# Linear attention and a gated MLP in one hand-ordered kernel: the third pair's alpha is loaded fifth of nine, and every engine's order is new

## The chip, the cores and the metric

The kernel runs on one core of a Trainium2 chip. The metric is the device time of one execution in microseconds (us); lower is better. TensorE (PE) multiplies matrices into PSUM, VectorE (DVE) and ScalarE (ACT) read PSUM, GpSimd (POOL) works on SBUF alone here, SyncE (SP) issues DMAs. Each engine takes its instructions in the program's order and waits on semaphores.

## The reference, cut to what matters

Eight heads of width 48, four batches of 768 tokens. A state of 48 x 48 per head is decayed by alpha on its rows and gets an outer product added, token by token; then all heads of a token form a row of 384 for an MLP whose gate is h cos(h).

```python
for t in range(S):
    state = alpha[:, :, t, :, None] * state + np.einsum('bhd,bhe->bhde', k[:, :, t], v[:, :, t])
    y[:, :, t] = np.einsum('bhd,bhde->bhe', q[:, :, t], state)
...
h = x @ w_in
g = h * np.cos(h)
return (g @ w_out).astype(np.float32)
```
x has 3072 rows of 384, d_ff is 2048.

## The kernel before, in words

**Tiles.** 256 tokens form a pair of chunks of 128; there are 12 pairs, J0 to J11, three to a batch. All matmuls take bf16. Two tokens stand on each partition (e is the token's parity), 64 partitions are one chunk (c).

**Steps of a pair.** `load` (L102) brings a (alpha), k, q, v from HBM on SP's queue, 384 KB each. For J0 to J2, `ln` (L140) takes the logarithm of alpha on ACT; `cums0` (L175) and `cums` (L159) sum logarithms up to each token with triangular matrices on TensorE, into two banks of PSUM; `icp` (L190) and `exps` (L195) take the exponentials of minus and plus these sums. From J3 on, `mula` (L148) first multiplies the two tokens' alphas on POOL, so only `cums` is needed (into a bank with the tag x), `sub` (L181) on DVE makes the other sum, and one step `eb`, the session (L203), does all four exponentials and the logarithm of the next pair. `sk` (L211) and `sq` (L215) multiply k and q by the exponentials, on POOL, or on DVE where the plan has :D. `trans` (L252) transposes the products on TensorE, `evT` (L262) copies them to SBUF (DVE, or ACT with :A), `scores` (L267) multiplies them, `mask` (L275) on DVE applies the causal mask. `outer` (L282), `add` (L299) and `state` (L309) carry the state on; `decay` (L241) makes the chunk's decay on POOL. `castv` (L219) makes v bf16 on POOL; `vpe` and `vev` (L231, L238), or `vst` with four DMAs (L222), put it into the order that `yT` needs. `yT` (L316) adds state and scores to y, transposed, and `evy` (L343) evicts it as the MLP's input.

**The MLP.** `m1` (L354) makes a quarter u of h on TensorE: 12 matmuls into two banks. `sin` (L363) takes the cosine on ACT, `gate` (L371) multiplies on DVE, `m2` (L376) multiplies by w_out in four parts for each half c of the pair, `evo` (L394) evicts, `store` (L404) writes 192 KB out.

**Resources that tie steps together.** PSUM has three slots of two banks (tag h: sums of J0 to J2, transposes, scores, outer products, y, quarters of h, in the order of their steps), one bank x (sums from J3 on, vpe), one bank o (m2's result and the filler). A step waits until the reader of the slot's last content is done. ACT has one set of functions for logarithm and exponential and another for the cosine; a change costs an ACT_TABLE_LOAD (L137, L366). The weights come on POOL's DMA queue, which casts them: w1 in two halves (L122: quarters 0 and 1, 2 and 3), w2 in four quarters (L127), one for each part of m2. `idle` (L411) is filler: matmuls of zeros into bank o.

**The order.** `PLAN` (L432) holds for each step and pair a due time in ns; the steps are issued in the order of these times (L502 to L515), which fixes each engine's order and each queue's. Nothing waits for the times themselves; a planner wrote them. `IDLE` (L500) places filler. `GATES` (L99) names a load that must wait for a step: alpha of J2 waits for the last matmul of yT J1, and all loads behind it on SP wait with it.

Of the kernel before, what the change touches and what calls it, by code (L numbers as in the profile page):

```python
# [16 lines left out]
def kernel(  # L17
# [11 lines left out]
    B, H, S, D = q.shape  # L29
# [64 lines left out]
    w1 = [consts.tile([C, KT, DF // 2], BF, tag=f"w1{r}", name="w1") for r in range(2)]  # L94
    w2 = consts.tile([C, NF, DM], BF, tag="w2", name="w2")

    a_sb, kqv, cp_sb, icp_sb, qkT_sb, A_sb, c2_sb = {}, {}, {}, {}, {}, {}, {}
    xT, gsb = {}, {}
    GATES, AFTER = {("a", 2): ("yT", 1)}, {}  # L99
    src = {"a": alpha, "k": k, "q": q, "v": v}  # L100

    def load(nm, J):  # L102
# [308 lines left out]
    def idle(n):  # L411
# [18 lines left out]


    PLAN = {  # L432
# [66 lines left out]
    }  # L499
    IDLE = [(1201, 9), (6413, 9), (9413, 4), (10803, 4), (11874, 5), (13469, 5), (15483, 4), (16533, 2), (17668, 1), (23484, 1)]  # L500

    order = []  # L502
    for key, line in PLAN.items():
        kind, *rest = key.split()
        for J, word in enumerate(line.split()):
            if word != "-":
                t, _, eng = word.partition(":")
                args = [J] + [int(x) if x.isdigit() else x for x in rest] + [{"A": "ACT", "D": "DVE", "P": "POOL"}[x] for x in eng]
                order.append((int(t), len(order), kind, args))
    for t, n in IDLE:  # L510
        order.append((t, len(order), "idle", [n]))
# [34 lines left out]
```

## Time and profile before

| | us |
|---|---|
| median of 3 runs | 186.08 (185.83 to 186.11) |
| the profiled execution | 185.2 |
| its span (first to last instruction) | 183.4 |
| first MLP matmul (m1 J0, quarter 1) | 20.62 |
| last matmul's group starts | 179.47 |
| TensorE busy in the span | 177.0 (96%) |
| filler on TensorE, 44 matmuls | 12.9 |
| ACT busy, table loads among it | 129.4, 18 of 1.28 each |

The page of the profile counts an engine as busy while an instruction of its own runs; matmuls overlap, and their ends are modelled, so starts are compared below. In a line of the time line stand the start, the time until the group's end, engine, source line, operation, what it writes and reads, the count, and in brackets the engine's idle time before it and what ended it. A line of waits has the total, the count and the longest. In a row of the table of stretches, the figures before (x...) are the busy us of PE, its weight loads, DVE, ACT and POOL; then the granted clock, the DMA engines' share and GB/s.

### The profile page before, as it was taken

The numbers are of one execution on the slowest core, as the hardware profiler recorded it, in microseconds if no ns is written. First come the engines' busy times: TensorE is split into PE (matmuls) and PEld (weight loads), VectorE is DVE, ScalarE is ACT, GpSimd is POOL, SyncE is SP. The second block draws the span as 40 slices with busy tenths as digits, with TensorE's granted clock in tenths as the row PEclk, the third lists the DMA queues.
The fourth block names the chain that finished last, engine by engine and source line by source line (L and its number), as shares of the span: only waits on it lengthen the run. The fifth ranks groups of instructions, "written<-read, shape, count | busy, mean of one in ns | idle before, by whom it ended". The sixth has DMA issues, their size and how long they took to land.

```text
span 183.4 us, 5752 instructions
## 1 busy us (share of the span) xinstructions
PE 177.0 (96%) x2473; PEld 132.8 (72%) x2473; DVE 128.4 (70%) x174; ACT 129.4 (71%) x168; POOL 80.3 (44%) x114
## 2 busy tenths in 40 slices
PE   7999999989999999989999999999999999999993
PEld 2444889664797876966789769776786796788772
DVE  7268879179889696689539985988569759074650
ACT  3665769698599989869798999659947173551531
POOL 5357500568687756562991099345075111000000
DMA  6999999999988999989228970571652300020122
GB/s 151 261 261 198 215 211 249 246 267 287 247 197 201 262 242 230 256 189 285 59 46 211 282 212 4 138 176 32 168 162 65 98 5 0 5 86 4 43 86 86
DMA packets 57801, 29.47 MB, mean 161 GB/s; under 512 B 50992, under 2 KB 56496, under 8 KB 57776
## 3 DMA queue, kind: packets, MB, share of 16 engines
q1 hardware_dynamic: 56256, 25.86, 57.7%
q0 software_dynamic: 1376, 3.15, 9.1%
q8 instruction: 19, 0.31, 0.7%
q10 hardware_dynamic: 144, 0.10, 0.2%
q14 instruction: 6, 0.05, 0.1%
HBM read 25.17 MB, written 4.72 MB: 163 GB/s over the span
## 4 chain that ended last, share of the span: by engine, by line
PE 87%; ACT 8%; DMA 2%; DVE 1%; issue 1%
PE h_ps L360 34%; PE o_ps L389 31%; PE y_ps L339 5%; PE A_ps L273 4%; PE idle_ps L415 3%; PE T_ps L259 3%; PE U_ps L290 2%; DMA a<-in_alpha_dram 2%; ACT c_sb L366 2%; ACT lna L142 2%; PE o_last L383 1%; ACT cp L201 1%; PE cums_h L156 1%; PE cums L156 1%; ACT icp L193 1%; ACT L137 1%
## 5 line engine op out<-in xcount | busy, mean ns | idle before, releaser
L371 DVE TENSOR_TENSOR gsb<-h_ps,c_sb 128x1024 bf16<-128x1024 f32 x48 | 58.1, 1222 | 24.1 <-ACT c_sb L366 22.8
L366 ACT ACTIVATE c_sb<-h_ps,halfpi 128x1024 bf16<-128x1024 f32 x48 | 52.8, 1113 | 24.1 <-PE h_ps L360 21.7
L389 PE MATMUL o_ps<-w,gsb 128*128 128x384 bf16 x368 | 67.4, 327 | 1.1 <-DVE gsb L371 0.8
L360 PE MATMUL h_ps<-xT,w 128*128 128x256 bf16 x576 | 67.1, 273 | 0.1
L360 PEld LDWEIGHTS <-w 128*128 128x128 bf16 x576 | 62.4, 114 | 2.7 <-issue 0.4
L389 PEld LDWEIGHTS <-gsb 128*128 128x128 bf16 x368 | 33.8, 98 | 22.1 <-DVE gsb L371 1.4
L312 POOL TENSOR_TENSOR un<-us,c 128x384 bf16<-128x384 f32 x20 | 16.7, 835 | 42.5 <-DVE us L304 27.6
L278 DVE TENSOR_TENSOR A_sb<-A_ps,msk 128x1024 bf16<-128x1024 f32 x24 | 28.8, 1216 | 2.7 <-PE A_ps L273 2.7
L217 POOL TENSOR_TENSOR qh<-q,cp 128x384 bf16<-128x384 f32 x21 | 20.9, 1004 | 12.3 <-PE A_ps L273 8.1
L213 POOL TENSOR_TENSOR kh<-k,icp 128x384 bf16<-128x384 f32 x17 | 17.0, 1006 | 0.7 <-ACT icp L193 0.7
L150 POOL TENSOR_TENSOR a<-a 128x384 f32<-128x384 f32 x9 | 9.0, 1000 | 15.0 <-DMA a<-in_alpha_dram 14.8
L415 PE MATMUL idle_ps<-zeros 128*128 128x512 bf16 x44 | 12.9, 428 | 1.2 <-DVE zeros L52 1.2
L265 DVE COPY qkT<-T_ps 128x1024 bf16<-128x1024 bf16 x14 | 9.3, 682 | 5.0 <-PE T_ps L259 5.0
L137 ACT ACT_TABLE_LOAD x9 | 11.5, 1283 | 0.9 <-PEq L530 0.7
L142 ACT ACTIVATE lna<-a 128x768 bf16<-128x768 f32 x12 | 10.1, 845 | 2.8 <-DMA a<-in_alpha_dram 2.8
L265 ACT COPY qkT<-T_ps 128x1024 bf16<-128x1024 bf16 x10 | 9.8, 1017 | 2.9 <-PE T_ps L259 1.6
L220 POOL CAST vp<-v 128x768 bf16<-128x768 f32 x12 | 9.9, 825 | 4.1 <-DMA v<-in_v_dram 4.1
L366 ACT ACT_TABLE_LOAD x9 | 11.5, 1283 | 0.2
L401 ACT COPY o_sb<-o_ps 128x384 f32<-128x384 f32 x12 | 5.8, 482 | 8.2 <-PE o_ps L389 8.2
L304 DVE TENSOR_TENSOR us<-U_ps,un 128x384 f32<-128x384 f32 x16 | 8.8, 551 | 2.5 <-PE U_ps L290 1.4
L350 ACT CAST xT<-y_ps 128x384 bf16<-128x384 f32 x14 | 7.6, 597 | 4.0 <-PE y_ps L339 3.4
L401 DVE COPY o_sb<-o_ps 128x384 f32<-128x384 f32 x11 | 6.1, 552 | 6.2 <-PE o_ps L389 6.2
(70 smaller groups left out, 153.1 us busy)
## 6 DMA issues: line engine op xcount, KB each, us to landing
a<-in_alpha_dram SPq DMA_DIRECT2D x12, 384.0 KB, 5.9
q<-in_q_dram SPq DMA_DIRECT2D x12, 384.0 KB, 5.4
k<-in_k_dram SPq DMA_DIRECT2D x12, 384.0 KB, 5.9
v<-in_v_dram SPq DMA_DIRECT2D x12, 384.0 KB, 5.9
out_dram<-o_sb SPq DMA_DIRECT2D x23, 192.0 KB, 2.1
vs<-vp SPq DMA_DIRECT2D x36, 64.0 KB, 2.5
w<-in_moe_w_in_dram POOLq DMA_DIRECT2D x2, 768.0 KB, 9.8
w<-in_moe_w_out_dram POOLq DMA_DIRECT2D x4, 384.0 KB, 9.1
```

What stands on the lines that cost most here:

```text
L137: nc.scalar.preload_act_table_set("natural_log_exp_and_others")
L142: nc.scalar.activation(out=lna_t[J % NL][:, :, :, 0:D].rearrange("p e h d -> p h e d"), in_=a_sb.pop(J), func=AF.Ln)
L213: eng.tensor_tensor(out=kh_t[J % NQ][:, e, :, 0:D], in0=kqv["k", J][:, :, e], in1=icp_, op=ALU.mult)
L217: eng.tensor_tensor(out=qh_t[J % NQ][:, e, :, 0:D], in0=kqv["q", J][:, :, e], in1=cp, op=ALU.mult)
L265: copy(out=qkT_sb[J][:, c], in_=T_ps[J][:, c].rearrange("r n e s -> r n (e s)"))
L278: nc.vector.tensor_tensor(out=A_sb[J][:, c].rearrange("s a p t -> s (a p) t"), in0=A_ps.pop((J, c)).rearrange("s a p t -> s (a p) t"), in1 ...
L312: nc.gpsimd.tensor_tensor(out=u, in0=U_sum.pop(n), in1=c2_sb[J][:, :, c].unsqueeze(3).to_broadcast([C, NP, 2, D]), op=ALU.mult)
L360: nc.tensor.matmul(h_ps[J, u][:, f, :], cols, xT[J][:, kk, :], start=(kk == 0), stop=(kk == KT - 1))
L366: nc.scalar.activation(out=c_sb[J, u], in_=h_ps[J, u], func=AF.Sin, bias=halfpi, scale=1.0)
L371: nc.vector.tensor_tensor(out=gsb[J][:, u * FW : (u + 1) * FW], in0=h_ps.pop((J, u)), in1=c_sb.pop((J, u)), op=ALU.mult)
L389: nc.tensor.matmul(o_ps[J, c][:, 0:DM], gsb[J][:, ft, c * C : (c + 1) * C], w2[:, ft], start=(ft == 0), stop=(ft == NF - 1))
L415: nc.tensor.matmul(idle_ps[0], zeros[:, 0:C], zeros, start=True, stop=True)
```

## The change

Only the order table changes: `PLAN`, `IDLE` and `GATES`. No function and no shape changes.

- Alpha of J2 is loaded fifth of nine loads at the start (a0, a1, q0, k0, a2, v0, k1, q1, v1); before, eight loads came first, and a2 with the later ones. Its logarithm, sums and exponentials stand among those of J0 and J1.
- The gate on yT J1 moves to alpha of J3.
- `ln` J3 now stands on ACT between two cosines of pair J1; before, it stood in the session of J2.
- TensorE has 41 matmuls of filler in place of 44; the one behind the first m1 is gone.
- Both halves of y of J0 and J1, and of some later pairs, are evicted next to each other on one engine.
- All later steps get new due times; some products and copies change engine (`sq` on DVE 11 times in place of 3, `sk` 9 in place of 7, `evo` 11 in place of 12).

The lines that the prediction speaks of, cut:

```diff
-    GATES, AFTER = {("a", 2): ("yT", 1)}, {}
+    GATES, AFTER = {("a", 3): ("yT", 1)}, {}
...
-        "load a": "750 1890 23566 24136 33206 39906 42906 54176 55781 57281 67081 74982",
+        "load a": "750 2205 4425 24496 25066 37693 43693 45193 55293 56793 62293 70470",
...
-        "w1": "11430 12280 45741 34391",
-        "w2": "19412 18392 21867 16762",
+        "w1": "12930 13780 14800 45594",
+        "w2": "18398 20198 24245 21048",
...
-        "ln": "4660 7660 31941 34779 - - - - - - - -",
-        "cums0": "5565 8565 33114 - - - - - - - - -",
+        "ln": "4660 6160 12304 35108 - - - - - - - -",
+        "cums0": "5565 7065 13604 - - - - - - - - -",
...
-        "icp 0": "6470 10760 33634 - - - - - - - - -",
-        "icp 1": "8400 10000 35519 - - - - - - - - -",
-        "exps 0": "6085 10375 34009 - - - - - - - - -",
-        "exps 1": "6845 9615 34394 - - - - - - - - -",
-        "eb": "- - - 40521 47404 57439 67428 82609 86208 101733 107581 125601",
+        "icp 0": "7285 8430 15799 - - - - - - - - -",
+        "icp 1": "8805 11929 15424 - - - - - - - - -",
+        "exps 0": "6900 7660 15039 - - - - - - - - -",
+        "exps 1": "8045 13044 14654 - - - - - - - - -",
+        "eb": "- - - 39444 47093 58049 68038 83323 88148 102153 108001 126061",
...
-        "m1 3": "23912 36576 53619 60672 74283 97913 108778 110096 134625 143522 159692 171168",
-        "sin 3": "25430 38196 55137 62190 75801 99431 111127 112135 136143 145040 161210 172686",
+        "m1 3": "24842 34044 54229 61582 76211 98333 109238 111209 134990 143887 160057 171533",
+        "sin 3": "26360 37142 55747 63100 77729 99851 111547 112727 136508 145405 161575 173051",
...
-    IDLE = [(1201, 9), (6413, 9), (9413, 4), (10803, 4), (11874, 5), (13469, 5), (15483, 4), (16533, 2), (17668, 1), (23484, 1)]
+    IDLE = [(1201, 9), (6413, 2), (7383, 14), (11727, 1), (12377, 4), (15372, 5), (16939, 5), (20459, 1)]
```

108 rows, old and new, of the table PLAN are left out of this document.

## The prediction, made before the changed kernel had run

> **What bounds the kernel now.** I read the page's busy times first, then the table of stretches, then TensorE's waits and time line, and then the landings of the DMAs that TensorE's first work needs.
>
> ```profile
> PE 177.0 (96%) x2473; PEld 132.8 (72%) x2473; DVE 128.4 (70%) x174; ACT 129.4 (71%) x168; POOL 80.3 (44%) x114
> ```
> ```profile
> 5.30:20.60 15.30, 15.09 (x238) 7.86 (x238) 9.66 (x14) 9.26 (x18) 8.27 (x12) 1.00 1.20 235
> ...
> 24.50:38.40 13.90, 13.90 (x117) 11.52 (x116) 8.24 (x10) 10.77 (x14) 4.13 (x5) 1.00 1.06 242
> 38.40:50.70 12.30, 11.16 (x225) 7.11 (x223) 10.87 (x15) 9.44 (x17) 8.46 (x11) 1.00 1.13 268
> 50.70:80.50 29.80, 29.79 (x417) 24.35 (x414) 24.09 (x29) 27.06 (x32) 21.20 (x26) 1.00 0.96 231
> ```
> TensorE (first busy figure) is full from 5.3 us on, but until 20.6 us much of it is filler (idle, L415). From the first MLP matmul at 20.62 us it only stops in the stretch 38.4 to 50.7. The DMA engines (share above 1.0 in the first 50 us) are just as full there. So the end is set by three things: when the first MLP matmul starts, how much work stands behind it, and the waits behind it. The granted clock is 1.00 in each row.
>
> ```profile
> 20.62 2.78 PE L360 MATMUL h_ps<-xT,w 128*128 128x256 bf16 x24
> ...
> 24.23 0.39 PE L415 MATMUL idle_ps<-zeros 128*128 128x512 bf16 x1
> 24.55 0.71 PE L360 MATMUL h_ps<-xT,w 128*128 128x256 bf16 x5
> ```
> ```profile
> PE o_ps L389 <- DVE gsb L371: 0.8, 1, 0.8
> PE T_ps L259 <- DVE gsb L371: 0.5, 1, 0.5
> PE o_ps L389 <- ACT o_sb L401: 0.3, 1, 0.3
> ```
> These three waits fall at 40.84, 80.95 and 44.69 us. The first and third come from pair 2's own session of logarithm and exponentials on ACT, which waits for alpha:
> ```profile
> 31.12 1.28 ACT L137 ACT_TABLE_LOAD   x1
> 32.79 0.84 ACT L142 ACTIVATE lna<-a 128x768 bf16<-128x768 f32 x1 [0.39 <-DMA a<-in_alpha_dram]
> 34.73 0.49 ACT L193 ACTIVATE icp<-cums_h 128x384 f32<-128x384 f32 x1 [1.09 <-PE cums_h L168]
> ...
> 37.12 1.28 ACT L366 ACT_TABLE_LOAD   x1
> 38.41 1.11 ACT L366 ACTIVATE c_sb<-h_ps,halfpi 128x1024 bf16<-128x1024 f32 x1
> ```
> The cosine of pair 1 at 38.41 waits behind that session, its gate on DVE behind it, and m2 at 40.84 behind the gate.
>
> **The change, step by step.** Pairs are J0 to J11; m1(J,u) and m2 are the MLP's matmuls.
>
> *1. The first m1: later by 0.6.* The eight input loads of before land at 4.39, 5.88, 7.39, 8.89, 10.40, 11.91, 13.43 and 14.98: one each 1.51 us. In the new order (a0 a1 q0 k0 a2 v0 k1 q1 v1) k1, q1 and v1 land one place later, v1 at 16.49. POOL casts v0 before it issues w1; v0 comes at 11.91 instead of 10.40, so w1 is issued 1.51 later too, and the weights queue behind inputs that end 1.51 later. In before the first half of w1 took 8.4 us from its issue at 11.22:
> ```profile
> w<-in_moe_w_in_dram POOLq DMA_DIRECT2D x1, 768.0 KB, 8.4
> ```
> so it landed at 19.64, and now at 21.15. TensorE's own chain is ready before that: fillers cost 0.213 us each plus 0.1 per group (9 of them: 6.16 to 8.26), which puts trans J0 at 10.2, cums J1 at 10.8, ln J2 at 11.9 to 12.6, its sums at 13.15 (when the exponential of J1 frees their bank), trans J1 at 16.2 (q1 lands at 14.98, then two DVE products of 0.55), yT J0 at 17.95 (18.66 in before), its evictions until 19.85, outer J1 at 19.9 (bank of y), vpe and a filler until 20.9. So m1(0,1) starts at 21.2 instead of 20.62: **+0.58**, the margin of the other chain being 0.3. m1(0,3) follows m1(0,1) by 3.93 in before (matmul, cosine, gate, then the bank is free); the filler at 24.23 stands inside that wait, so taking it out is worth 0.
>
> *2. Pair 2's sums before the first m1.* cums0 and cums of J2 occupy TensorE from 33.70 to 34.55. They now stand where filler stood: **-0.85**. The load that J2's alpha waited for (the gate on yT J1) now holds J3's alpha; the same number of loads stands ahead of J3's k, q and v, so these land where they did (41.3, 42.8, 45.3). J2's q, k, v land 1.5 later (37.1, 38.5, 39.9); trans J2 needs them at 40.9, so nothing waits. All loads behind on SP keep their distance.
>
> *3. The waits from 24.5 to 52 us.* Before, measured by starts against neighbours: 0.79, 0.29 and 0.31 (at 40.84, 42.44 and 44.69), 1.39 in sum. After:
> - m2(0,0) part 2 needs the last quarter of w2. It landed at 31.68, now 33.2, and TensorE asks for it at 33.0: 0.2 to 0.4, I take 0.3 (bounds 0 and 1).
> - m1(1,3) moves ahead of J0's last m2, so nothing covers that eviction: 36.50 (m2) to 37.91 (copy ended) in before, 1.45 from start to a free bank, less the 0.65 of the m2 itself: 0.8. In before m1(1,3) hid it.
> - J3's alpha lands at 34.4, POOL's product ends at 35.5, ln at 36.3, cosine (1,3) at 37.6, session J3 at 39.95 to 42.3. vpe J2 needs the bank that these exponentials read until 41.65, and comes at 41.85: 0 as long as the two waits above stand; 0.4 if they go, so they trade places.
> - From there ACT is the tight engine: two evictions of J2, two of T, session J4 at 47.2 to 49.5, two of y until 50.55; m1(2,1) at 50.6, where TensorE would be at 50.4: 0.2.
>
> Sum 1.3 against 1.39: **-0.09**. At J2's second m1 that gives 51.9 instead of 52.29.
>
> On one term a rule speaks against the change. A table load takes 1.28 us, and each order has 18. The Trainium skill, ScalarE: Activation LUTs, "Table sets: the hidden batching unit", says to do all functions of one set before switching. J3's logarithm now stands alone between two cosines and needs two loads for 0.85 us of work. By the rule, ACT would be 2.6 us earlier with it elsewhere and the 0.2 above would be 0; by the row the sum stands.
>
> The weights meet the loads of J3, J4 and q2, issued at 24.8 as before, while 1.5 us more of the weights is left. In before, from 24 to 30 us the input queue moved 512 packets and 0.20 MB beside 1.10 MB of weights. The Trainium skill, DMA: Bandwidth & Descriptors, "Queues, rings and completion order", has each engine go round its queues packet by packet; those counts agree. By it the last weights lose 0.65 us more of sharing, some 0.1 us, and the sum is -0.56 instead of -0.66.
>
> *4. The rest, 52 us to the end.* Same instructions in another order; table loads 9 and 9 in both. Behind J2's second m1 the old order changes 44 times between the MLP's matmuls or sums and attention's, the new one 42 times; a change costs 0.09 in the trace (m2 to m2 0.65, m2 to scores 0.74), so -0.2. The wait at 80.95 came from POOL's product for J6 ending at 80.90, behind a cast that waited for v6 until 76.40:
> ```profile
> 76.40 0.82 POOL L220 CAST vp<-v 128x768 bf16<-128x768 f32 x1 [2.09 <-DMA v<-in_v_dram]
> ...
> 79.89 1.00 POOL L213 TENSOR_TENSOR kh<-k,icp 128x384 bf16<-128x384 f32 x1
> ```
> ```profile
> 80.95 0.41 PE L259 MATMUL T_ps<-ident_bf,kh 64*128 64x64 bf16 x16 [0.46 <-DVE gsb L371]
> ```
> (The wait is put down to the gate that ended at 80.94 as well; by the order of the slots, trans took the one that the gate before it had freed at 79.63.) Now DVE makes that product, so 0.46 goes. But with the order new everywhere, waits of this size appear at places that I can't see: from none to two of them, 0 to 1.0 us. So this stretch is worth -0.66 to +0.34; I take 0.36 of new waits, a little less than the one that goes: **-0.3**.
>
> Sum: +0.58 - 0.85 - 0.09 - 0.3 = -0.66. The profiled execution took 185.2 (span 183.4 and 1.8 around it): 184.5. The median of 186.08 lies 0.9 above that execution, so **185.4**; own range 185.0 to 185.7.
>
> **Rivals.**
> - *Nothing gained: new waits take it back.* vpe's wait of 0.4 for the bank of J3's session stands beside the others instead of in their place, and the stretch behind 52 us is near its upper end: -0.36 + 0.4 + 0.3, 186.4. For it: ACT is at 27.1 of 29.8 from 50.7 us on, with little room. Against: in before trans J6 is the only step behind 52 us with a wait in the profile.
> - *Slower: the weights come later than the shift of 1.51.* The place is the one line of DMA: nine loads, w1, w2, alpha of J3. 0.2 MB of w1 got through beside the last inputs in before; without that, at 0.2 MB per us, w1 lands 1.0 later, and the first m1, m2's last quarter, and the chain from J3's alpha through ln and the session move with it. It decides from 1.0 us on: 0.66 is eaten up, and over 0.2% slower follows. At 2 us: 187.4; at 1.1: 186.5. For it: the weights already end late (31.68). Against: issue and inputs move by the same 1.51.
> - *More gained: no new waits behind 52 us, and none of 0.2 at m1(2,1):* -0.36 - 0.2 - 0.66, 184.9.
> - *It doesn't do what it says:* ln J2 late, sums after the first m1. Its alpha lands at 10.4, ACT is free at 11.9; I give it nothing.
>
> **How the numbers follow.** Forecast 0.45, more gained 0.12, nothing gained 0.23, slower 0.20. 0.2% is 0.37 us, about what a measurement of this kernel can tell from no change. Forecast and more gained lie below 185.7: faster 0.57. Of nothing gained and the edge of slower, 0.22 is within; 0.21 slower. The range takes in both sides: 184.6 to 187.0.
>
> **What would show it.** The first h_ps at 21.2, released by w's DMA; no sums of J2 after it; the cosine (1,3) alone between two table loads at 36 to 39; a wait of 0.8 for the copy of o near 39; J2's first m1 near 50.6; trans J6 without wait. Wrong would be: a first h_ps later than 22, m2 waiting for w2 by over 1 us, or over 1 us of new waits behind 52 us.

## The result: 0.8% faster, twice what was forecast

| | median us (range, runs) | ratio to before on the same chip, 95% interval |
|---|---|---|
| before, beside the first run of after | 185.78 (184.87 to 186.11, 6) | |
| after | 184.04 (183.84 to 184.52, 6) | 0.992 [0.9891, 0.9948] |
| after, second time | 183.85 (183.32 to 185.51, 9) | 0.9916 [0.9889, 0.9943] |
| after, third time | 183.86 (183.48 to 184.06, 6) | 0.9932 [0.9918, 0.9946] |

The forecast was 185.4 with a range from 184.6 to 187.0; the time came out below the range. The profiled execution of after took 184.12 (span 182.3). The lines that answer to those of before, first the page's busy times:

```profile
PE 175.4 (96%) x2467; PEld 132.6 (73%) x2470; DVE 134.8 (74%) x183; ACT 129.9 (71%) x169; POOL 71.4 (39%) x104
```
and the table of stretches of after:

```profile
5.30:20.60 15.30, 14.36 (x239) 8.20 (x242) 10.07 (x15) 9.83 (x21) 7.39 (x11) 1.00 1.22 238
...
24.50:38.40 13.90, 13.74 (x152) 11.53 (x141) 9.53 (x10) 11.74 (x12) 3.93 (x6) 1.00 1.12 240
38.40:50.70 12.30, 11.64 (x230) 7.46 (x228) 10.67 (x14) 11.66 (x21) 9.02 (x11) 1.00 1.18 261
50.70:80.50 29.80, 29.80 (x414) 24.43 (x413) 24.58 (x30) 27.69 (x34) 13.99 (x18) 1.00 1.00 240
```
TensorE is busy 1.6 us less in all, 0.73 of it between 5.3 and 20.6 us, where it has less filler and stops more. Between 38.4 and 50.7 us it now stops for 0.66 instead of 1.14. Where the MLP begins, its time line of after says:

```profile
20.35 0.52 PE L290 MATMUL U_ps<-vp,kh 64*128 64x96 bf16 x16 [0.32 <-ACT xT L350]
20.80 0.35 PE L235 MATMUL vs_ps<-vp,ident_bf 64*64 64x384 bf16 x2
21.30 2.88 PE L360 MATMUL h_ps<-xT,w 128*128 128x256 bf16 x24 [0.16 <-issue]
...
25.24 2.03 PE L360 MATMUL h_ps<-xT,w 128*128 128x256 bf16 x17 [0.16 <-DVE gsb L371]
```
The first m1 stands at 21.30. TensorE's waits of after that answer to those shown, and the largest new one behind the start:

```profile
PE o_ps L389 <- DVE o_sb L401: 0.6, 1, 0.6
PE A_ps L273 <- DVE gsb L371: 0.5, 1, 0.5
```
The wait of 0.8 for a gate at 40.84, that of 0.3 for a copy on ACT and that of trans J6 are gone. The first line is the copy of o that nothing covers (m2 at 39.38), the second the scores of J5 at 83.09. ACT's time line of after, where pair 2's session had been:

```profile
33.78 1.28 ACT L137 ACT_TABLE_LOAD   x1
35.27 0.84 ACT L142 ACTIVATE lna<-a 128x768 bf16<-128x768 f32 x1 [0.20 <-POOL a L150]
36.13 1.28 ACT L366 ACT_TABLE_LOAD   x1
37.42 1.11 ACT L366 ACTIVATE c_sb<-h_ps,halfpi 128x1024 bf16<-128x1024 f32 x1
38.56 1.28 ACT L137 ACT_TABLE_LOAD   x1
39.85 0.52 ACT L193 ACTIVATE icp<-cp 128x384 f32<-128x384 f32 x1
```
J3's logarithm stands alone between two loads, the cosine (1,3) behind it, and the session of J3 starts at 39.85 (39.95 was forecast).

**A common zero.** Executions differ in when the first transfer lands: the first alpha at 4.37 to 4.67 us, and with it all that follows. Counted from that landing, the profiled executions read:

| | first alpha lands | first m1 | J2's second m1 | trans J6 | last m2 group |
|---|---|---|---|---|---|
| before | 4.39 | 16.23 | 47.90 | 76.56 | 175.08 |
| before, second time | 4.60 | 16.22 | 47.89 | 76.86 | 175.44 |
| after | 4.67 | 16.63 | 46.90 | 77.29 | 173.74 |
| after, second time | 4.63 | 16.67 | 46.92 | 77.31 | 173.73 |
| after, third time | 4.54 | 16.63 | 46.96 | 77.36 | 173.79 |

(trans J6 has another place in the new order.) After is the same three times within 0.07; the gain is 1.34 against the first execution of before and 1.70 against the second. The medians give 1.3 to 1.6 (0.0068 to 0.0084 of about 185.5). The spans on the pages (183.4 and 182.3) show only 1.1, because the profiled before had its first alpha 0.28 earlier than the profiled after.

### The profile page after: what moved, and what is told of

Read it like the earlier page. It is cut to its first block, busy times and chain, and to the rows that moved or that the text cites. A ratio compares the mean times of both kernels' runs of the same rounds, so it can differ in the third digit from the quotient of the medians.

```text
span 182.3 us, 5756 instructions
## 1 busy us (share of the span) xinstructions
PE 175.4 (96%) x2467; PEld 132.6 (73%) x2470; DVE 134.8 (74%) x183; ACT 129.9 (71%) x169; POOL 71.4 (39%) x104
## 4 chain that ended last, share of the span: by engine, by line
PE 77%; ACT 11%; DVE 6%; DMA 2%; issue 2%; ACTq 0%
PE h_ps L360 29%; PE o_ps L389 28%; PE y_ps L339 5%; DVE gsb L371 5%; PE idle_ps L415 4%; ACT c_sb L366 3%; PE A_ps L273 3%; PE T_ps L259 3%; DMA a<-in_alpha_dram 2%; PE U_ps L290 2%; ACT L366 2%; PE o_last L383 1%; ACT L137 1%; ACT lna L142 1%; PE cums_h L156 1%
## 5 line engine op out<-in xcount | busy, mean ns | idle before, releaser
L312 POOL TENSOR_TENSOR un<-us,c 128x384 bf16<-128x384 f32 x20 | 16.8, 838 | 46.2 <-DVE us L304 36.9
L217 POOL TENSOR_TENSOR qh<-q,cp 128x384 bf16<-128x384 f32 x13 | 13.8, 1063 | 13.3 <-ACT cp L201 12.2
L213 POOL TENSOR_TENSOR kh<-k,icp 128x384 bf16<-128x384 f32 x15 | 14.9, 1007 | 2.4 <-ACT icp L193 1.0
L415 PE MATMUL idle_ps<-zeros 128*128 128x512 bf16 x38 | 11.1, 439 | 1.4 <-DVE halfpi L77 1.2
L217 DVE TENSOR_TENSOR qh<-q,cp 128x384 bf16<-128x384 f32 x11 | 6.8, 629 | 5.4 <-DMA q<-in_q_dram 5.3
L273 PE MATMUL A_ps<-qkT 48*128 48x128 bf16 x192 | 9.0, 217 | 0.7 <-DVE gsb L371 0.5
```

The costliest lines, as they stand in the source:

```text
L213: eng.tensor_tensor(out=kh_t[J % NQ][:, e, :, 0:D], in0=kqv["k", J][:, :, e], in1=icp_, op=ALU.mult)
L217: eng.tensor_tensor(out=qh_t[J % NQ][:, e, :, 0:D], in0=kqv["q", J][:, :, e], in1=cp, op=ALU.mult)
L273: nc.tensor.matmul(A_ps[J, c][:, a, p, :], qkT[r, c, NP + p, :], qkT[r, c, p, :], start=True, stop=True)
L312: nc.gpsimd.tensor_tensor(out=u, in0=U_sum.pop(n), in1=c2_sb[J][:, :, c].unsqueeze(3).to_broadcast([C, NP, 2, D]), op=ALU.mult)
L415: nc.tensor.matmul(idle_ps[0], zeros[:, 0:C], zeros, start=True, stop=True)
```

## The experiments

Each kernel has the order table of before or of after with the edit that is named; "old" and "new" order mean these. Each ratio is to before, measured beside the run on the same chip. In the text from here on, the times of the first m1, J2's second m1, trans J6 and the last m2 count from the landing of the first alpha, as in the table above; all other times, and those in the lines shown, count from the start of the span.

**1. Which half of the order brings it.** The tables were cut at 52.9 us (52.3 for the reverse), the rest of the steps put behind in the other table's order.

```
h1: steps due before 52.9 us as after, all later ones in the order of before
h2: steps due before 52.3 us as before, all later ones in the order of after
```


> The changed order up to the fourth-last quarter of J2's first MLP step (all steps due before 52.9 us in its own plan), then the old order for all that is left. By the traces the front is worth 0.72 of the 1.06 us between the two profiled executions (second m1 of J2 at 51.57 instead of 52.29). Theory A, front and back each bring their part and the old order has a wait behind 52 us that comes and goes (its executions spread from 184.87 to 186.11): 0.7 us faster than before, with a spread of about 1 us still there, and trans J6 late as in before. Rival B, the part that comes and goes lies in the old front (J2's alpha behind the weights): 1.3 to 1.7 us faster, spread under 0.7 us.

> The old order up to the same place in the program, then the changed order. Theory A: 0.3 us from the back's own order and some 0.5 to 0.7 more because the wait that comes and goes is gone: 0.8 to 1.0 faster, spread under 0.7 us. Rival B: 0.2 to 0.4 faster, spread as wide as in before.

> The changed kernel once more, beside the two halves on one chip. Both theories: 1.5 us faster than before (ratio 0.992), its first m1 at 21.2 to 21.4.

> The kernel before once more, for a second profile of it and for the spread of its times. If its profiled execution is one of the slow ones of its spread (185.7 or more), the place where its time line lags behind the first profile's shows where the spread comes from: behind 52 us by theory A (POOL's cast of v6 and trans J6, or a wait further back), before 52 us by rival B (J2's alpha and the steps behind it).

h1: 184.49 (184.11 to 185.99, 12 runs), 0.9954 [0.9934, 0.9973]: the front half brings 0.85 us (0.5 to 1.2), as theory A has it. In its trace J2's second m1 stands at 46.95, as in after, and the last m2 at 174.06. h2: 187.15 (186.16 to 190.06, 8 runs), 1.0086 [1.0049, 1.0123], which neither theory had. Its profiled execution took 190.06, 2.9 above its median; the wait is plain in it:

```profile
PE T_ps L259 <- POOL qh L217: 2.5, 1, 2.5
```
```profile
58.76 1.00 POOL L150 TENSOR_TENSOR a<-a 128x384 f32<-128x384 f32 x1 [2.61 <-DMA a<-in_alpha_dram]
...
59.89 1.00 POOL L217 TENSOR_TENSOR qh<-q,cp 128x384 bf16<-128x384 f32 x1
```
At the seam POOL has a later pair's alpha to multiply before J4's q, waits 2.61 for its load, and trans J4 waits 2.5 for POOL. Late in that wait the granted clock of TensorE fell to 0.50 for 6.8 us, and the 12 matmuls of m2 there took 4.02 us (2.12 in before, at 58.38):

```profile
60.25:67.08 6.83, 6.13 (x40) 3.25 (x41) 4.38 (x6) 2.58 (x4) 3.15 (x4) 0.50 0.88 186
```
```profile
61.43 4.02 PE L389 MATMUL o_ps<-w,gsb 128*128 128x384 bf16 x12
```
So h2 measures the seam, not the back half: no run here measures the new order's back half behind the old front. The second run of before (185.31, 0.9987 [0.997, 1.0003]) shows what in the old order varies:

```profile
81.46 0.41 PE L259 MATMUL T_ps<-ident_bf,kh 64*128 64x64 bf16 x16 [0.76 <-POOL kh L213]
```
The wait of trans J6 was 0.46 in the first execution and 0.76 here, now put down to POOL's product, because v6 came 0.5 later (POOL's cast 76.92 instead of 76.40).

**2. The lead alone, and the trades behind it.**

```
h3: steps due before 24.9 us as after, all later ones in the order of before
a2 (on after):  "cums" J3  36668 -> 37900    "sub" J3  38162 -> 38700
a3 (on after):  "ln" J3  35108 -> 38100   "cums" J3 -> 38800   "sub" J3 -> 39000
```


> The new order for the steps due before 24.9 us (input order, pair 2's logarithm, sums and exponentials early, the first matmuls of the MLP), the old order for all that follows. Theory A (the early sums and the late first m1 give -0.85 + 0.68, and the lost waits of 0.56 come because pair 2's session no longer stands between the MLP's steps, whatever the order of the rest): J2's second m1 comes 0.5 to 0.8 earlier than in before, the median is 0.4 to 0.9 below before's. Rival R (the waits are lost by the new placement of J3's logarithm, sums and session between 33 and 42 us): only the sums' net -0.17 is seen at J2's second m1, the waits are still 1.2 to 1.4 in sum, and the median is within 0.3 of before's.

> The new order with J3's sums behind pair 0's last m2 instead of ahead of it, and the subtraction on DVE behind the eviction, so that 0.4 us of matmuls cover the wait of 0.8 for the copy of o. Theory A (the wait trades with the bank that J3's exponentials read: vpe J2 stands at 41.7 with almost no room, as the prediction says): the wait for the copy falls to 0.4, vpe J2 waits 0.3 to 0.5 instead, and the median stays within 0.2 us of the new order's. Rival R (they don't trade, since TensorE has other work there): the median falls by 0.3 to 0.45.

> The new order with J3's logarithm, its sums and its subtraction moved behind the cosine (1,3), into J3's session: one pair of table loads less (2.57 us of ACT). Theory A (the chain cosine, load, logarithm, sums, subtraction, exponentials is as long as before, since the 1.28 of a load between 36.1 and 37.4 makes room for the sums' way over TensorE and DVE): the session starts at 39.8 to 40.3 instead of 39.85, J2's first m1 within 0.3 of where it is, the median within 0.3 us of the new order's. Rival R (the rule of the Trainium skill, ScalarE: Activation LUTs, Table sets: the hidden batching unit, that one does all functions of a set before switching, holds for the time too): the session starts 1 us or more earlier and the median falls by 0.3 or more.

h3: 185.25, 0.9995 [0.998, 1.001]. The rival holds: the early sums and the input order alone bring nothing. TensorE's time line of h3 shows why:

```profile
35.35 2.76 PE L389 MATMUL o_ps<-w,gsb 128*128 128x384 bf16 x16 [0.65 <-DVE o_sb L401]
...
44.74 0.81 PE L389 MATMUL o_ps<-w,gsb 128*128 128x384 bf16 x4 [0.32 <-ACT o_sb L401]
```
In before J2's sums stood just where J0's first copy of o was awaited, and covered it. Taken away, they leave a wait of 0.65 (0.8 by starts) at 35.35; in exchange the wait of 0.79 at 40.84 for the gate is gone, since no session of J2 holds up the cosine. The waits of 0.3 at 42.4 and 44.7 stay. The new order from 25 to 52 us then moves m1(1,3) onto the first copy, leaves the second copy bare, and loses the two of 0.3: J2's second m1 stands at 47.78 in h3, at 46.95 in h1.

a2: 183.81 (183.56 to 184.09, 6 runs), 0.992 [0.9902, 0.9938], as the new order. Theory A holds in kind:

```profile
PE o_ps L389 <- DVE o_sb L401: 0.4, 1, 0.4
...
PE vs_ps L235 <- ACT cp L201: 0.2, 1, 0.2
```
The wait for the copy falls from 0.65 to 0.41 and vpe J2, which had come just in time, waits 0.18 for the bank that J3's exponentials read (0.3 to 0.5 was expected). a3: 184.34, 0.9953 [0.9935, 0.9971], by medians 0.3 to 0.5 us above the new order's three (the intervals of the ratios overlap a little). With one pair of table loads less, the session starts at 40.65 instead of 39.85, 1.0 later counted from the first alpha:

```profile
38.25 0.84 ACT L142 ACTIVATE lna<-a 128x768 bf16<-128x768 f32 x1
40.65 0.52 ACT L193 ACTIVATE icp<-cp 128x384 f32<-128x384 f32 x1 [1.56 <-DVE cp L183]
```
ACT saves 2.57 us of loads, and then waits 1.56 for the way of the sums over TensorE and DVE, which after hides behind the cosine (1,3). J2's second m1 comes 1.0 later (47.89), the end only 0.3 (174.03). The Trainium skill, ScalarE: Activation LUTs, "Table sets: the hidden batching unit", would have all functions of a set done before a switch; the trace disagrees for the time here, since the order with two loads more has J2's matmuls 1.0 earlier. So neither theory holds: theory A had put the session 0.35 too early and J2's first m1 within 0.3 of its place.

**3. What holds the start.**

```
a4 (on after):  "w1" first half  12930 -> 8700   IDLE without (20459, 1)
a6 (on after):  the same with 8800, "sq 0" J0 on POOL (8700) and a memset of a spare tile ahead of w1
b3 (on before): IDLE (13469, 5) -> 3, (16533, 2) -> 1, (17668, 1) gone
b4 (on before): b3 with "sk 0" J6  77541 -> 77541:D
```


> The new order with the first half of w1 issued on POOL before v0's cast instead of behind it (some 3 us earlier), and without the filler at 20.459. Theory A (the first m1 at 21.30 stands behind both w1 at 20.98 and attention's chain, outer J1 and vpe at 20.80 to 21.1): with w1 out of the way and the filler gone it comes at 21.0 to 21.1, and the weights behind it land earlier too: 0.2 to 0.3 us faster than the new order. Rival R (the weights take the DMA engines from k1, q1 and v1, which land 0.5 to 1.5 later, and trans J1 with them): the first m1 comes at 21.5 to 22.5, and the time rises by 0.2 to 1.2 us.

> The new order with w1's first half issued on POOL at some 11.3 us, ahead of v0's cast, but just behind the start of v1's load at 11.7 (a product of q0 and a memset of a spare tile stand on POOL ahead of it, the filler at 20.459 is gone); with it 1.1 us earlier still it had cost 7 us, because v1's load, which then started 0.7 behind w1's, landed at 24.71 instead of 16.55. Theory A (what counts is which transfer starts first: a load that starts ahead of the weights keeps its 1.51 us): v1 lands at 16.3 to 17, w1's first half at 19.3 to 20, the first m1 comes 16.2 to 16.5 us behind the landing of the first alpha instead of 16.65, the last quarter of w2 lands 0.5 to 1.5 earlier, and the median falls by 0.1 to 0.5 against the new order's. Rival R (the weights' packets take their share of what is left of every load): v1 lands at 18 to 24, trans J1's values follow, and the time is 1.5 us or more above the new order's.

> The old order without four of its fillers ahead of the first m1 (five become three at 13.469, two become one at 16.533, the one at 17.668 goes), some 0.9 us of TensorE. Theory A (the old order's start hangs on TensorE's own chain, the fillers in it, and on no DMA; the line of DMA is met only at trans J6, where v6's cast on POOL is late): the first m1 stands 15.4 to 15.9 us behind the landing of the first alpha instead of 16.2, J2's first m1 is as much earlier, and then the wait at trans J6 grows by most of it, so that the median falls by 0 to 0.3 only. Rival R (the start of the old order hangs on w1 or on q1, k1 and v1): the first m1 stays within 0.2 of 16.2 and the median within 0.2 of before's. A second rival (nothing behind takes it back): 0.4 to 0.8 faster.

> The same with sk 0 of J6 on DVE, so that trans J6 doesn't wait for POOL behind v6's cast. Theory A: the two act together where neither does much alone: no wait at trans J6, 0.4 to 0.9 us faster than before. Rival R (trans J6 is not what takes it back): as the run without this edit, within 0.2 us.

a4: 190.87, 1.0289 [1.0257, 1.0321]. The rival holds, far beyond its size. From the DMA issues of a4 from 9.5 to 12.5 us (the last figure is us to landing), and POOL's time line:

```profile
w<-in_moe_w_in_dram POOLq DMA_DIRECT2D x1, 768.0 KB, 9.9
q<-in_q_dram SPq DMA_DIRECT2D x1, 384.0 KB, 6.2
v<-in_v_dram SPq DMA_DIRECT2D x1, 384.0 KB, 14.6
```
```profile
24.76 0.82 POOL L220 CAST vp<-v 128x768 bf16<-128x768 f32 x1 [7.42 <-DMA v<-in_v_dram]
```
A transfer's start is taken here as the end of the instruction that issues it. v1's transfer started 0.7 behind w1's (11.49 and 10.78). It landed at 24.71, behind both halves of w1; q1, which had started at 10.05, kept its time (14.85). TensorE stood 5.6 us at vpe, and its granted clock was 0.50 from 24.3 us, late in that wait, to 31.1 us, so the 7 us by which a4 is slower are not the late v1 alone. a6 put w1's start at 11.88, 0.33 behind v1's at 11.55: v1 landed at 16.34, as theory A has it, but w1's first half only at 20.36 (19.3 to 20 was expected). Counted from the first alpha that is 0.32 earlier than in after, though w1 was issued 1.8 earlier. And the product that I moved to POOL stood beside DVE's for k0, so that trans J0 waited:

```profile
11.11 0.38 PE L263 MATMUL T_ps<-ident_bf,kh 64*128 64x64 bf16 x14 [0.66 <-DVE kh L217]
```
The first m1 came at 17.23 instead of 16.63. The median is 184.05, 0.9935 [0.9916, 0.9954], as the new order: at the end (173.77) nothing of those 0.6 is left.

b3: 184.85, 0.9973 [0.9958, 0.9987]. The first m1 comes at 15.62 instead of 16.23, so the old start hung on TensorE's own chain with its filler, and 0.5 us of the median is to be had without the change. What takes the early start back is not what theory A named. J2's alpha landed no earlier, and its sums waited for the logarithm:

```profile
33.98 0.32 PE L156 MATMUL cums_h<-lna,tri 128*128 128x384 bf16 x1 [0.50 <-ACT lna L142]
```
By J2's second m1 (48.12) 0.83 is gone, more than the start had gained. Trans J6, whose wait theory A saw grow, has no wait in this trace, and the last m2 comes at 174.77, 0.31 ahead of before's first execution. b4: 184.88, 0.44 below before's median, but the ratio is 0.9993 [0.9978, 1.0009], so it is inconclusive. In the traces trans J6 waits in neither b3 nor b4, and a gain on top of b3 isn't shown.

**4. The stretch behind 52 us.**

```
b2 (on before): "sk 0" J6  77541 -> 77541:D
c1 (on h1):     the same edit
a8 (on after):  "mula" J9  74420 -> 76500 (on POOL behind the cast of v6)
a9:             a8 and a2 together
```


> The old order with one edit: sk 0 of pair J6, POOL's last product ahead of trans J6, goes to DVE, as in the new order. Theory A (the gain of the new order behind 52 us is mostly the wait of trans J6 for POOL, which in the profiled execution of before was 0.46 us, and in another execution of the same program 1.0): DVE can make the product in the gap of 1.33 ahead of its gates or just behind them, trans J6 starts 0.4 to 0.6 earlier, the wait for POOL is gone, and the median falls by 0.4 to 0.9 us against before. Rival R (that wait only moves on: the steps behind it wait for something else, and the gain behind 52 us is spread over the whole order): within 0.25 us of before, and the first steps behind trans J6 wait for ACT or DVE instead.

> The new order up to 52.9 us and the old one behind it, with sk 0 of J6 on DVE. Theory A (what the new order gains behind 52 us is the wait of trans J6 for POOL, 0.40 in the run without this edit): the time behind J2's second m1 falls from 127.1 to 126.6 to 126.9, as in the new order, and the median comes within 0.25 us of the new order's. Rival R (it is something else, fewer changes for one): the median stays at that of the run without this edit, 0.4 to 0.7 above the new order's, and the wait turns up elsewhere.

> The new order with POOL's product for J9's alpha (77.13 to 78.13 in the trace of after) moved behind the cast of v6. In after DVE's two products for J6 stand beside it and beside that cast, and take 0.88 and 1.18 us instead of 0.55; the gates behind them end late, and TensorE waits 0.49 for one at 83.09. Theory A (the wait of 0.49 comes from DVE being held up beside POOL): DVE's first product takes 0.55, the second 0.55 to 0.9, the gates start 0.4 to 0.8 earlier, the wait at scores J5 falls to 0 to 0.1, and the time behind J2's second m1 falls from 126.8 by 0.3 to 0.5; the median by 0.2 to 0.5. Rival R (DVE's times there have another cause, or the gates wait for the cosines anyway): the wait stays at 0.4 to 0.5, the median within 0.2 of the new order's.

> The same together with J3's sums behind pair 0's last m2 (the run in which the wait for the copy of o fell to 0.41 and vpe J2 waited 0.18, and the wait at scores J5 was gone). If the wait at scores J5 is the only thing that the two have in common, the two don't add up: within 0.2 us of the first of them. If the sums' place is worth something by itself: 0.2 to 0.4 faster than the first.

> The new order once more, as the yardstick of this call: a ratio of 0.990 to 0.994 to before, the first m1 16.6 to 16.7 us behind the landing of the first alpha, J2's first m1 at 45.6 and the last m2 at 173.7 behind it.

b2: 185.41 (184.9 to 186.29, 12 runs), 1.0006 [0.9991, 1.0022]: no gain, although DVE makes the product in time and trans J6 follows without a wait:

```profile
81.29 0.41 PE L259 MATMUL T_ps<-ident_bf,kh 64*128 64x64 bf16 x16
```
In that execution the start was slow: the four matmuls of J0's sums took 1.23 us (5.52 to 6.75) where before's took 0.65 (5.31 to 5.96), the first m1 came at 16.86, and trans J6 at 76.69, between before's two. In before a late start may be partly taken up by the wait for v6's cast, which goes by the line of transfers; taking the wait away would then save only what the late start hadn't used up. That is my reading of this one execution; why the median of 12 runs doesn't fall isn't shown. c1: 184.21, 0.995 [0.9933, 0.9968], between h1 and after, and 0.35 above the after measured beside it. Trans J6 doesn't wait, but the sums of J8 and trans J11 do, 0.22 and 0.27, and trans J3 ahead of them 0.27. So that wait is not all that the new order gains there. The rest is no wait at all: TensorE's own work behind J2's second m1 is 0.5 shorter in the new order, as step 4 below shows.

a8: 183.90 (183.41 to 184.78, 8 runs), 0.9938 [0.9913, 0.9962], as the after measured beside it. Its profiled execution settles where the wait at scores J5 comes from. DVE's time line of after, then of a8:

```profile
77.67 0.88 DVE L213 TENSOR_TENSOR kh<-k,icp 128x384 bf16<-128x384 f32 x1
78.47 1.18 DVE L217 TENSOR_TENSOR qh<-q,cp 128x384 bf16<-128x384 f32 x1
79.56 3.47 DVE L371 TENSOR_TENSOR gsb<-h_ps,c_sb 128x1024 bf16<-128x1024 f32 x3
```
```profile
77.64 0.55 DVE L213 TENSOR_TENSOR kh<-k,icp 128x384 bf16<-128x384 f32 x1
78.11 0.55 DVE L217 TENSOR_TENSOR qh<-q,cp 128x384 bf16<-128x384 f32 x1
78.58 3.52 DVE L371 TENSOR_TENSOR gsb<-h_ps,c_sb 128x1024 bf16<-128x1024 f32 x3
```
and POOL's beside them, of after, then of a8:

```profile
77.13 1.00 POOL L150 TENSOR_TENSOR a<-a 128x384 f32<-128x384 f32 x1
78.39 0.84 POOL L220 CAST vp<-v 128x768 bf16<-128x768 f32 x1 [0.26 <-DMA v<-in_v_dram]
```
```profile
78.56 0.82 POOL L220 CAST vp<-v 128x768 bf16<-128x768 f32 x1 [1.96 <-DMA v<-in_v_dram]
```
With POOL idle both products take 0.55, the gates start 1.0 earlier, the wait of 0.49 is gone, and J2's second m1 to the end takes 126.14 instead of 126.83. In a9 v6 landed earlier, POOL's cast and product stood beside DVE's again, the first product took 1.30, and a wait of 0.32 came back (184.14, 0.9944 [0.9925, 0.9962], 0.24 above a8; its first sums were slow too, and its first m1 came at 17.02). So the mechanism is shown in the traces, and by them it bites or not with the time at which v6 lands. That may be why a8's median doesn't show what its trace does; it wasn't tested. No version that I ran is measurably faster than after.

## Why the prediction was wrong, point by point

The direction was right, and so were most of the places; the sum was half of what came, and the shift onto the median was wrong. Of -0.66 forecast, the traces make -1.34 by the common zero, first execution against first. Forecast and median lie 1.36 apart (185.4 and 184.04): 0.9 of that is the shift, and most of the rest the error of the sum (0.68), less the 0.28 by which the first alpha of the profiled after came later.

- **Step 1, the first m1, +0.58: right in kind, 0.17 too large.** 16.23 became 16.63: +0.41, in all of after's executions and in h1 and h3 (16.63 to 16.69). The shift of 1.51 for w1's first half holds; the place that it started from was the late end of a spread. Counted from the first alpha, it landed at 14.8 to 15.3 in the traces with the old start, at 15.25 in the one that the prediction used, and at 16.3 to 16.8 in those with the new start (a4 and a6 aside); 16.76 was forecast, and after had 16.31. It lands (20.98) as TensorE's own chain ends (vpe from 20.80 on), so either can hold the first m1.
- **Step 2, the sums, -0.85: right as a term, but not free.** The lead as a whole brought 0 in h3: the sums had covered J0's first copy of o. I had counted one bare copy (0.8) in step 3, so the total holds only together with m1(1,3) moving onto the first copy.
- **Step 3, the waits from 24.5 to 52 us, -0.09: this is the step of the sum that failed.** Measured -0.55: the first m1 to J2's second m1 took 31.67 before and 30.27 after, 1.40 less, of which 0.85 are the sums. Two terms that I had put down as waits weren't there. The 0.3 for w2's last quarter: it landed at 33.03 (33.2 forecast), and TensorE asked for it at 33.10 (33.0 forecast). Counted from the first alpha the quarter came 1.08 later than in the first execution of before, not 1.5, and it came just in time, by 0.07. The 0.2 of the ACT chain: the evictions of y ended at 50.21 instead of 50.55, and m1(2,1) began at 50.26 directly behind TensorE's own work. The 0.8 for the bare copy was right. So was the 0 for vpe's bank, though one of the two waits that it rested on didn't come: the session was 0.4 earlier too, counted from the first alpha. a2 shows the trade that the step named.
- **Step 4, behind 52 us, -0.3: right in its total by the trace, which is partly luck.** -0.34 against the first execution of before, -0.71 against the second. The wait of 0.46 went, as forecast. Of new waits I had taken 0.36, and 0.64 came (0.49 at scores J5, 0.15 at outer J8). TensorE's own work I had put 0.2 shorter, for two changes less; it is 0.5 shorter. The stretch from J2's second m1 to the last m2 group, of before, then of after (length, then TensorE's busy time):

```profile
52.29:179.47 127.18, 126.69 (x1787) 99.43 (x1785) 91.05 (x104) 92.44 (x115) 54.56 (x67) 1.00 0.52 131
```
```profile
51.57:178.41 126.84, 126.20 (x1785) 99.39 (x1784) 96.96 (x113) 90.90 (x112) 45.54 (x58) 1.00 0.52 134
```
In the eight traces with the old order there (before twice, b2, b3, b4, h1, h3, c1) TensorE is busy for 126.6 to 126.8 us, in the eight with the new one (after three times, a2, a3, a6, a8, a9) for 126.0 to 126.2. Why the same matmuls take that much less in the new sequence isn't shown. So b2 and c1, which take only the wait at trans J6 away, leave this part of the gain behind.
- **The shift onto the median, +0.9: wrong, and the largest part of the miss.** I added the 0.9 by which the median of 3 runs lay above the profiled execution. The old order's medians in more runs were 185.1 to 185.8, so the median of 3 was high, and the profiled execution (185.2) was no unusual one. What varies between its executions is seen in the traces: the first landing, slow first sums, the wait at trans J6. The new order has no wait at trans J6. Slow sums it passes on in part: in after's three executions they took 0.65 to 0.94 us and the first m1 stays within 0.04, but in a9, whose edits lie behind 36 us, they took 1.24 and the first m1 came at 17.02. In the old order 0.65, 0.80 (h2) and 1.23 us (b2) went with a first m1 at 16.23, 16.38 and 16.86. How the 0.9 is shared among these wasn't measured. After's profiled execution (184.12) lies 0.1 from its median.
- **The rivals.** "More gained" was nearest: its sum, -1.22, is close to the measured -1.34. One of its two reasons held, no wait of 0.2 at m1(2,1); the other, no new waits behind 52 us, did not, and it had no place for w2's quarter or for work that is shorter by more than 0.2. "Weights later than the shift" fell: counted from the first alpha, w1 came 0.45 earlier than forecast in after, and in none of the other traces with its start later. a4 shows the reverse of it on the same line of DMA, a load of the inputs that starts behind the weights, and the price there is 7 us.

## What to carry to other kernels

When work is taken from the engine that bounds, look first at what that work was covering: h3 took 0.85 us away and got a wait of 0.8 back. A wait forecast from two times that lie within 0.2 us of each other is a coin toss and belongs into the range, not into the sum. Before a profiled time is carried onto a median, fix a common zero in the traces, and ask whether the change keeps what makes the executions differ. And where waits don't explain a difference, compare the busy time of the engine that bounds: here a part of the gain was no wait.

## What the runs showed of the hardware

- **Order of transfers.** An input of 384 KB that started 0.7 us behind a cast transfer of the weights took 14.6 us from issue to landing instead of 6.2 (a4); ahead of it by 0.33 us it kept its time (a6). The weights' queue moved its first packet at 13.72 us in before, 15.17 in after, 15.05 in a6 and 13.84 in a4: 1.2 to 3.2 us behind the end of their first issue, and in each case 1.0 to 1.4 us ahead of the landing of the last input that had started before them. So a6's earlier issue gained little; why the weights wait isn't shown. Once both run they share: in a4 from 16 to 24.5 us the input queue moved 980 packets and 0.37 MB, the weights' queue 597 packets and 1.16 MB, and in before from 24 to 30 us the packets were 512 and 408. The Trainium skill, DMA: Bandwidth & Descriptors, "Queues, rings and completion order", has an engine go round its queues packet by packet; 1.6 and 1.3 small packets for one large one are nearer to that than to equal bytes. Whether what it calls a packet is what the profile counts isn't shown.
- **DVE beside POOL.** DVE's product of 0.55 took 0.88, 1.18 and 1.30 us beside work of POOL, and POOL's cast of 0.82 took 1.15 beside them in the second execution of after. The Trainium skill, Trainium Architecture — The Big Picture, "What this means for kernel authors", calls the port pair of the two an exclusive lock; the trace agrees: each of these three products ends 0.40 to 0.42 us behind the end of POOL's instruction beside it (78.55 and 78.13, 79.65 and 79.23 in after, 79.41 and 79.01 in a9), whatever its own length.
- **The start.** The four matmuls of J0's sums took 0.65 us in before and 1.23 in b2. The traces' records of the granted clock go with it. All traces but before's have such a record; its first grant of 1.0 stands at 3.9 to 5.4 us where the sums took 0.65, and at 5.6 to 7.2 us where they took longer. Within a trace the matmuls that began ahead of the grant took 0.35 to 0.52 each, and those behind it 0.32 to 0.33 (after: grant at 6.07, matmuls of 0.48, 0.43, 0.33 and 0.33 from 5.58 on). The column of the clock in the tables of stretches says 1.00 there all the same, as it counts time ahead of the first record as full.
- **The clock behind a long wait.** Late in TensorE's wait of 2.5 us in h2 and in that of 5.6 us in a4 the granted clock fell to 0.50, and stayed there for 6.8 us. In no other trace does TensorE wait over 0.9 us behind its first 5 us, and none has a clock under 1.00 between the first grant and the last matmul.
